# A delta-rule attention with two MoE layers on one core: last second products of a block issued ahead of the next block's first products, and three smaller edits around them

## The chip, the core and the metric

The kernel runs on one core of a Trainium2 chip. Its engines work from queues of their own: TensorE (PE, with its weight loads as PEld), VectorE (DVE), ScalarE (ACT), GpSimd (POOL) and SyncE (SP), which here only issues DMAs. The metric is the device time of one execution in microseconds; lower is better.

## What is computed

The inputs are q, k, v (4 batches, 8 heads, 768 steps, 48 wide), beta, and four weight matrices. All is float32.

```python
k_n = k / (norm(k) + 1e-06)
for t in range(S):                       # state: B, H, 48, 48
    y[:, :, t] = q[:, :, t] @ state
    v_old = k_n[:, :, t] @ state
    state += beta[:, :, t] * outer(k_n[:, :, t], v[:, :, t] - v_old)
x = y.transpose(0, 2, 1, 3).reshape(3072, 384)
h = x @ w_in                             # 384 -> 2048
x = (h * tanh(softplus(h))) @ w_out      # 2048 -> 384, "MoE1"
h = x @ w_in2
out = (h * clip(h + 3, 0, 6) / 6) @ w_out2   # "MoE2"
```

## The kernel before

**Order.** The program for all engines is one static order. `Flow.run` makes it: every part of the work is a generator that yields what it needs next (an event by name, or an engine and a planned duration), and the planner, with a virtual clock for each engine, lets the part with the earliest start plus its penalty (`pen`) go on. The planner's durations are the numbers in the code, such as 0.62 for a cast on ACT. On the chip every engine then runs its list in that order, and waits at semaphores.

**Attention.** The 768 steps are 24 chunks of C = 32, t = 0 to 23. Per chunk, `rec` chains the state products (`S_mm`, L769), the products with it (L719: `ksps` for k, `yps` for q), U (`U_pe`, L729: `ups`, copied to the tile `u` by ACT at L860), MU (`MU_pe`, L739: M times u on top of `yps`) and X (L913, a transpose into the operand of MoE1, copied to `xst` at L929). U needs the inverse of a triangular matrix per chunk and head. For chunks 0 to 7 `quads(0)` and `quads(1)` make these inverses four chunks at a time, and finish them in groups of chunks `ts` with products Q (L626, `qps`); the later ones come from `substs` (L677, L684 on DVE).

**MoE.** `moe` runs 192 units: u = 0 to 95 are MoE1, 96 to 191 MoE2; 6 blocks of 512 tokens times KF = 16 units of 128 hidden columns in each. The first product of a unit (`mm1`, L1080) is 9 matmuls 128x512. Float32 precision is made from split operands: x is xh + xl and w is wh + wl, and the products are xh·wh, xl·wh, xh·wl for each of KD = 3 thirds. The result `hps` goes through the activation function (L1111, or L1207 and L1209 in MoE2), is split into `ghi` (L1086, ACT) and `glo` (L1120 on POOL in MoE1, L1215 on DVE in MoE2), and enters the second product (`mm2`), of 9 matmuls 128x512 (L1101) in MoE1 and 12 matmuls 128x384 (L1234) in MoE2. `mm2` of unit u-2 stands behind `mm1` of unit u. After a block's last `mm2`, `flush1` writes its result to DRAM for MoE2, and `flush2` writes the output: four copies (DVE and ACT, two each) and then four DMAs, one for each batch (L1254).

**Operand of the next block.** `make_x` makes xh (three casts on ACT, L1058) and xl (three subtractions on DVE, L1062) of block n. There is one pair of tiles for xh and xl, so the first cast waits until the last `mm1` of block n-1 is done. Casts and subtractions are asked for in turn: cast 0, subtraction 0, cast 1, and so on.

**Weights.** Raw weights of both layers are converted piece by piece: four steps and the cut of the high part on DVE (L1010 to L1025), the high part as a cast on ACT (L1042, `wih`, `woh`), the low part as a subtraction on DVE (L1045, `wil`, `wol`). MoE1's pieces are converted during the start-up and block 0, those of MoE2 from the end of the attention on.

**Fillers.** `warm` issues matmuls whose result nobody reads, where the planner sees PE idle: 512 columns at L1388 until the first `mm1`, then 256 columns at L1396 until `mm1` of unit 15. Those of L1396 write one bank and wait each for the one before.

**Activation table.** ACT loads the table for the MoE1 function ahead of time (`mish`, L1378).

Of the kernel before, what the change touches and what calls it, by code (L numbers as in the profile page):

```python
# [8 lines left out]
F32 = mybir.dt.float32  # L9
# [117 lines left out]
def tile_delta_rule__moe_mish__moe_hardswish(  # L127
# [38 lines left out]
    with tc.manual_schedule():  # L166
# [408 lines left out]
        def quads(i):  # L575
# [37 lines left out]
            for ts in ((0,), (1,), (2, 3)) if i == 0 else ((0, 1), (2, 3)):  # L613
# [172 lines left out]
        def rec():  # L786


            for t in range(NS):
# [66 lines left out]
                if t:  # L856
                    yield f"MU{t - 1}"
                yield "ACT", 0.5
                u = ut[t] = ap_.tile([128, H, D], F32, tag="u", name="u")
# [191 lines left out]
        def make_x(n, src, last):  # L1051

            if last is not None:
                yield f"mm1.{last}"
            xhl[n] = x = [xp.tile([128, KD, 512], F32R, tag=f"x{p}", name=f"x{p}") for p in "hl"]
            for kk in range(KD):
                yield "ACT", 0.62
                nc.scalar.activation(out=x[0][:, kk, :], in_=src[:, kk, :], func=ACTF.Copy)  # L1058
                if kk == 0 and last is not None:
                    yield 0.8  # L1060
                yield "DVE", 0.55
                nc.vector.tensor_tensor(out=x[1][:, kk, :], in0=src[:, kk, :], in1=x[0][:, kk, :].bitcast(F32),  # L1062
                                        op=ALU.subtract)
                if kk == 0:
                    at = flow.cur
            flow.set(f"mx{n}")
            flow.ev[f"xk{n}"] = at
# [86 lines left out]
        def moe():  # L1154
# [8 lines left out]
            flow.set("moe1")  # L1163
            for u in range(2 * NB * KF):
# [19 lines left out]
                if u >= 2:  # L1184
                    yield from (mm2_second if u - 2 >= NB * KF else mm2_first)(u - 2)
            for u in range(2 * NB * KF - 2, 2 * NB * KF):
                yield from mm2_second(u)
# [52 lines left out]
        def flush2(n):  # L1240
# [3 lines left out]
            for s in range(4):  # L1244
                yield ("DVE", 0.45) if s % 2 else ("ACT", 0.5)
                if s % 2:
                    nc.vector.tensor_copy(out=o[:, s, :], in_=a[s])
                else:
                    nc.scalar.activation(out=o[:, s, :], in_=a[s], func=ACTF.Copy)
            flow.set(f"flush{n}")  # L1250
            yield "SP", 0.3
            for b in range(B):
                r0 = b * S + 128 * i
                nc.sync.dma_start(  # L1254
                    out=out[r0:r0 + 128, :].rearrange("(t s) d -> s t d", s=C),
                    in_=o[C * b:C * (b + 1)],
                )
# [205 lines left out]
```

## Time and profile before

| | us |
|---|---|
| device time, median of 3 runs (lowest, highest) | 1095.82 (1094.92, 1096.76) |
| device time of the profiled execution | 1095.95 |
| its span, first to last instruction | 1094.2 |
| first `mm1` of MoE1 starts | 110.56 |
| first `mm1` of unit 13 starts | 197.32 |
| first `mm1` of MoE2 starts | 674.78 |
| last copy of the output begins | 1087.90 |
| mean granted TensorE clock, share of full | 0.991 |

In a row of the timeline the columns are start, duration, engine, line, operation, output and inputs, shapes, the number of instructions in the row, and in brackets the idle time of the engine just before and what ended it. "128x512 f32 x3" means three such instructions. A matmul's duration is longer than the distance to the next one, since they are pipelined; distances are taken from start to start.

### The profile page before, as it was taken

How to read it: one execution, taken by the hardware profiler on the slowest of the kernel's cores; microseconds unless marked ns; L12 is line 12 of the kernel's file. 1: busy time of each engine (PE TensorE's matmuls, PEld its weight loads, DVE VectorE, ACT ScalarE, POOL GpSimd, SP SyncE). 2: the span in 40 equal slices, each digit the busy share in tenths (PEclk: the TensorE clock that was granted, in tenths of full speed). 3: DMA queues.
4: the chain of work that ended last, by engine and by line, in shares of the span. 5: the costliest groups of instructions: out<-in, count | busy, mean ns of one | idle time of the engine just before them, and what ended most of it. 6: DMA issues, size and time to landing. Idle time of an engine off the chain costs nothing.

```text
span 1094.2 us, 30690 instructions
## 1 busy us (share of the span) xinstructions
PE 1055.4 (96%) x13294; PEld 870.9 (80%) x13329; DVE 664.7 (61%) x1554; ACT 419.0 (38%) x822; POOL 208.3 (19%) x215
## 2 busy tenths in 40 slices
PE   8888999999999999999999998999999999999997
PEld 4666788777778787887887786898989989889896
DVE  6777888868496586938743899834333343333432
ACT  3334544434353344343323434433333342333332
POOL 3110343232333324232322332000000000000000
PEclk9999999999999999999999998999999999999999
DMA  6352434132423333231212543202002020020101
GB/s 150 87 147 51 140 87 112 31 72 38 80 44 74 61 61 82 40 65 28 66 22 73 162 127 116 102 1 58 1 1 58 1 58 1 1 59 1 30 1 29
DMA packets 145799, 66.05 MB, mean 60 GB/s; under 512 B 129760, under 2 KB 132832, under 8 KB 145664
## 3 DMA queue, kind: packets, MB, share of 16 engines
q1 hardware_dynamic: 143456, 63.65, 24.1%
q8 instruction: 104, 1.70, 0.7%
q10 hardware_dynamic: 2208, 0.44, 0.2%
q14 instruction: 31, 0.25, 0.1%
HBM read 50.43 MB, written 13.63 MB: 59 GB/s over the span
## 4 chain that ended last, share of the span: by engine, by line
PE 78%; DVE 16%; issue 2%; ACT 2%; DMA 1%; SPq 1%; POOL 0%; ACTq 0%; DVEq 0%; POOLq 0%
PE hps L1080 30%; PE p L1234 17%; PE o L1101 12%; PE warm L1388 3%; DVE tmp L677 3%; DVE tp L684 3%; PE dsps L769 3%; PE gps L427 2%; PE tps L407 2%; DVE xl L1062 2%; PE qps L626 2%; PE yps L739 1%; PE ups L729 1%; PE ksps L719 1%; PE yps L719 1%
## 5 line engine op out<-in xcount | busy, mean ns | idle before, releaser
L1080 PE MATMUL hps<-xl,wih 128*128 128x512 f32 x576 | 229.3, 398 | 9.8 <-DVE xl L1062 9.8
L1080 PE MATMUL hps<-xh,wih 128*128 128x512 f32 x576 | 229.4, 398 | 6.7 <-ACT g L1111 3.5
L1080 PE MATMUL hps<-xh,wil 128*128 128x512 f32 x576 | 227.1, 394 | 0.0
L1120 POOL TENSOR_TENSOR glo<-g,ghi 128x512 fp32r<-128x512 f32 x96 | 132.5, 1380 | 327.2 <-ACT ghi L1086 273.4
L1209 DVE SCALAR_TENSOR_TENSOR r<-r,hps 128x512 f32<-128x512 f32 x96 | 66.0, 688 | 174.5 <-ACT r L1207 174.5
L1207 ACT ACTIVATE r<-hps,half_c 128x512 f32<-128x512 f32 x96 | 66.1, 689 | 186.7 <-PE hps L1080 186.7
L1080 PEld LDWEIGHTS hps<-xl,wih 128*128 128x128 f32 x576 | 108.4, 188 | 36.4 <-DVE xl L1062 18.1
L1111 ACT ACTIVATE g<-hps 128x512 f32<-128x512 f32 x96 | 57.1, 595 | 197.9 <-PE hps L1080 187.9
L1080 PEld LDWEIGHTS hps<-xh,wih 128*128 128x128 f32 x576 | 108.5, 188 | 30.6 <-ACT g L1111 4.0
L1234 PE MATMUL p<-woh,glo 128*128 128x384 f32 x384 | 129.5, 337 | 0.0
L1234 PE MATMUL p<-woh,ghi 128*128 128x384 f32 x384 | 129.3, 337 | 0.0
L1234 PE MATMUL p<-wol,ghi 128*128 128x384 f32 x384 | 129.0, 336 | 0.0
L1080 PEld LDWEIGHTS hps<-xh,wil 128*128 128x128 f32 x576 | 108.5, 188 | 22.3
L677 DVE TENSOR_TENSOR tmp<-tp,ash 128x126 f32<-128x126 f32 (+22 forms) x248 | 100.8, 406 | 39.1 <-DMA ash<-ad 23.7
L1101 PE MATMUL o<-ghi,woh 128*128 128x512 f32 x288 | 114.7, 398 | 0.0
L1101 PE MATMUL o<-ghi,wol 128*128 128x512 f32 x288 | 114.2, 397 | 0.0
L1215 DVE TENSOR_TENSOR glo<-r,ghi 128x512 fp32r<-128x512 f32 x96 | 66.5, 693 | 59.3 <-ACT ghi L1086 58.8
L684 DVE TENSOR_TENSOR tp<-tp,tmp 128x126 f32<-128x126 f32 (+22 forms) x248 | 82.2, 332 | 7.5 <-DVE tmp L677 0.3
L1086 ACT ACTIVATE ghi<-r 128x512 fp32r<-128x512 f32 x96 | 60.6, 632 | 67.1 <-DVE r L1209 67.0
L1101 PE MATMUL o<-glo,woh 128*128 128x512 f32 x288 | 84.5, 395 | 0.0
L781 DVE TENSOR_TENSOR sbd<-sbd,dsps 48x192 f32<-48x192 f32 x152 | 53.5, 352 | 38.6 <-PE dsps L769 35.4
L1234 PEld LDWEIGHTS p<-woh,ghi 128*128 128x128 f32 x384 | 72.2, 188 | 4.2
(138 smaller groups left out, 1430.1 us busy)
## 6 DMA issues: line engine op xcount, KB each, us to landing
raw<-in_moe_w_in_dram SPq DMA_DIRECT2D x24, 512.0 KB, 4.0
raw<-in_moe_w_out_dram SPq DMA_DIRECT2D x32, 384.0 KB, 3.3
vt<-in_v_dram SPq DMA_DIRECT2D x96, 48.0 KB, 2.2
qpad<-in_q_dram SPq DMA_DIRECT2D x96, 48.0 KB, 2.3
x2d<-x2out SPq DMA_DIRECT2D x6, 768.0 KB, 3.8
x2in<-x2d SPq DMA_DIRECT2D x6, 768.0 KB, 6.0
out_dram<-osb SPq DMA_DIRECT2D x24, 192.0 KB, 3.2
ash<-ad SPq DMA_DIRECT2D x16, 256.0 KB, 3.9
```

The lines of the kernel that those rows point to most:

```text
L677: nc.vector.tensor_tensor(out=tv, in0=x[:, 0:m, j:j + 1].to_broadcast([128, m, n]), in1=a[:, j + 1:C, j:j + 1].rearrange("p i o -> p o i") ...
L684: nc.vector.tensor_tensor(out=x[:, 0:m, j + 1:C], in0=x[:, 0:m, j + 1:C], in1=tv, op=ALU.add)
L781: nc.vector.tensor_tensor(out=o, in0=o, in1=S_part(b, r), op=ALU.add)
L1080: nc.tensor.matmul(out=ps[0], lhsT=w[:, kk, c], rhs=xhl[n][xi][:, kk, :], start=(kk == 0 and x == 0), stop=(kk == KD - 1 and x == 2))
L1086: nc.scalar.activation(out=hi, in_=g, func=ACTF.Copy)
L1101: nc.tensor.matmul(out=acc[i][dc], lhsT=w[:, e, 128 * dc:128 * (dc + 1)], rhs=a, start=(f == 0 and x == 0), stop=(f == KF - 1 and x == 2))
L1111: nc.scalar.activation(out=g, in_=ps, func=ACTF.Mish)
L1120: nc.gpsimd.tensor_tensor(out=lo, in0=g, in1=hi.bitcast(F32), op=ALU.subtract)
L1207: nc.scalar.activation(out=r, in_=ps, func=ACTF.Relu, scale=1.0 / 6.0, bias=half_c)
L1209: nc.vector.scalar_tensor_tensor(out=r, in0=r, scalar=1.0, in1=ps, op0=ALU.min, op1=ALU.mult)
L1215: nc.vector.tensor_tensor(out=lo, in0=r, in1=hi.bitcast(F32), op=ALU.subtract)
L1234: nc.tensor.matmul(out=acc[n][s], lhsT=a[:, c], rhs=w[:, e, :], start=(f == 0 and x == 0), stop=(f == KF - 1 and x == 2))
```

## The change

Five places are edited. (1) In `quads(0)` the chunks 2 and 3 are finished one by one and no longer as a pair. (2) In `rec` the copy of U into `u` waits for the MU product of the chunk before only from chunk 4 on; chunks 1 to 3 put it in tiles of the tag `ghi` instead of the one tile `u`. (3) In `make_x` the three casts are asked for one behind another, and each subtraction is a part of its own that begins when its cast is placed. (4) In `moe` a counter `done` replaces the fixed distance of two units: behind `mm1` of a block's first and last unit, second products are issued up to the unit before, else up to two units before. (5) `flush2` issues one DMA for each of the four copies, directly behind it, in place of the four per batch behind all copies.

```diff
@@ quads @@
-            for ts in ((0,), (1,), (2, 3)) if i == 0 else ((0, 1), (2, 3)):
+            for ts in ((0,), (1,), (2,), (3,)) if i == 0 else ((0, 1), (2, 3)):
@@ rec @@
-                if t:
+                if t >= 4:
                     yield f"MU{t - 1}"
                 yield "ACT", 0.5
-                u = ut[t] = ap_.tile([128, H, D], F32, tag="u", name="u")
+                if 0 < t < 4:
+                    u = gp.tile([128, 512], F32, tag="ghi", name="u")[:, 0:H * D].rearrange("p (h d) -> p h d", h=H)
+                else:
+                    u = ap_.tile([128, H, D], F32, tag="u", name="u")
+                ut[t] = u
                 nc.scalar.activation(out=u, in_=ups.pop(t), func=ACTF.Copy)
@@ make_x @@
-            for kk in range(KD):
-                yield "ACT", 0.62
-                nc.scalar.activation(out=x[0][:, kk, :], in_=src[:, kk, :], func=ACTF.Copy)
+            left, at = [KD], []
+
+            def low(kk):
                 if kk == 0 and last is not None:
                     yield 0.8
                 yield "DVE", 0.55
                 nc.vector.tensor_tensor(out=x[1][:, kk, :], in0=src[:, kk, :], in1=x[0][:, kk, :].bitcast(F32),
                                         op=ALU.subtract)
-                if kk == 0:
-                    at = flow.cur
-            flow.set(f"mx{n}")
-            flow.ev[f"xk{n}"] = at
+                left[0] -= 1
+                at.append(flow.cur)
+                if not left[0]:
+                    flow.set(f"mx{n}")
+                    flow.ev[f"xk{n}"] = at[0]
+
+            for kk in range(KD):
+                yield "ACT", 0.62
+                nc.scalar.activation(out=x[0][:, kk, :], in_=src[:, kk, :], func=ACTF.Copy)
+                flow.add(low(kk), pen=-0.2)
@@ moe @@
+            done = -1
             for u in range(2 * NB * KF):
...
-                if u >= 2:
-                    yield from (mm2_second if u - 2 >= NB * KF else mm2_first)(u - 2)
-            for u in range(2 * NB * KF - 2, 2 * NB * KF):
-                yield from mm2_second(u)
+
+                while done < u - (1 if f in (0, KF - 1) else 2):
+                    done += 1
+                    yield from (mm2_second if done >= NB * KF else mm2_first)(done)
+            while done < 2 * NB * KF - 1:
+                done += 1
+                yield from mm2_second(done)
@@ flush2 @@
+                r0 = 128 * i + C * s
+                nc.sync.dma_start(out=out.rearrange("(b n) d -> b n d", b=B)[:, r0:r0 + C, :], in_=o[:, s, :])
             flow.set(f"flush{n}")
-            yield "SP", 0.3
-            for b in range(B):
-                r0 = b * S + 128 * i
-                nc.sync.dma_start(
-                    out=out[r0:r0 + 128, :].rearrange("(t s) d -> s t d", s=C),
-                    in_=o[C * b:C * (b + 1)],
-                )
```

Since the planner makes the order anew, instructions move in other places too. The lines below L610 shift: L1080 is L1090 in the changed kernel, L1101 is L1111, L1396 is L1405, L1042 is L1046, L1058 is L1076, L1062 is L1066, L1111 is L1121 and L1086 is L1096.

**PE in block 0, between `mm2` of unit 6 and `mm1` of unit 9.** Before:

```order
L1101 MATMUL o_2542<-glo,woh_2238 128x512 [waits Pool_49]
L1101 MATMUL o_2543<-glo,woh_2238 128x512
L1101 MATMUL o_2544<-glo,woh_2238 128x512
L1080 MATMUL hps<-xh,wih_2675 128x512 [waits Activation_49]
L1080 MATMUL hps<-xl,wih_2675 128x512
L1080 MATMUL hps<-xh,wil_2676 128x512
```

And now:

```order
L1111 MATMUL o_2457<-glo,woh_2232 128x512 [waits Pool_49]
L1111 MATMUL o_2458<-glo,woh_2232 128x512
L1111 MATMUL o_2459<-glo,woh_2232 128x512
L1405 LDWEIGHTS ident
L1405 MATMUL warm<-ident 128x256 [waits DVE_49]
L1405 LDWEIGHTS ident
L1405 MATMUL warm<-ident 128x256 [waits PE_49]
```

The last two rows repeat until there are 35 such fillers, and then `mm1` of unit 9 follows. Further groups of 7, 5 and 1 stand ahead of `mm1` of units 11 and 13 and later in the block. Before there were 8 ahead of `mm1` of unit 3, 2 ahead of that of unit 13 and 1 ahead of that of unit 16: 11 in all, and 48 now. Of the fillers at the old L1388 (L1397 now) there were 206, and 197 now.

**PE at the switch from block 0 to block 1 of MoE1.** The rows begin with the last matmul of `mm2` of unit 13. Before:

```order
L1101 MATMUL o_2544<-glo,woh_4041 128x512
L1396 LDWEIGHTS ident
L1396 MATMUL warm<-ident 128x256 [waits Activation_49]
L1080 MATMUL hps<-xh,wih_916 128x512 [waits PE_49,Activation_49]
L1080 MATMUL hps<-xl,wih_916 128x512 [waits DVE_49]
L1080 MATMUL hps<-xh,wil_917 128x512
L1080 MATMUL hps<-xh,wih_916 128x512 [waits Activation_49]
L1080 MATMUL hps<-xl,wih_916 128x512 [waits DVE_49]
```

And now:

```order
L1111 MATMUL o_2459<-glo,woh_4115 128x512
L1111 MATMUL o_2457<-ghi,woh_4115 128x512 [waits Activation_49]
L1111 MATMUL o_2457<-ghi,wol_4116 128x512 [waits DVE_49]
L1111 MATMUL o_2458<-ghi,woh_4115 128x512
L1111 MATMUL o_2458<-ghi,wol_4116 128x512
L1111 MATMUL o_2459<-ghi,woh_4115 128x512
L1111 MATMUL o_2459<-ghi,wol_4116 128x512
L1111 MATMUL o_2457<-glo,woh_4115 128x512 [waits Pool_49]
L1111 MATMUL o_2458<-glo,woh_4115 128x512
L1111 MATMUL o_2459<-glo,woh_4115 128x512
L1090 MATMUL hps<-xh,wih_916 128x512 [waits Activation_49]
L1090 MATMUL hps<-xl,wih_916 128x512 [waits DVE_49]
```

`mm2` of unit 14 has moved ahead of `mm1` of unit 16. Behind it come `mm2` 15, `mm1` 17, `mm1` 18 and `mm2` 16. The ten other switches are alike.

**ACT ahead of the first operand of MoE2.** `woh` and `wih` are converted weights of MoE2, `xh` the operand's high part, `g` and `ghi` those of the last units of MoE1. Before:

```order
L1111 ACTIVATE g<-hps 128x512
L1042 ACTIVATE woh_10623<-cw 128x384
L1086 ACTIVATE ghi<-g 128x512
L1042 ACTIVATE woh_10623<-cw 128x384
L1058 ACTIVATE xh<-x2in 128x512
L1111 ACTIVATE g<-hps 128x512
L1086 ACTIVATE ghi<-g 128x512
L1058 ACTIVATE xh<-x2in 128x512 x2
```

And now:

```order
L1046 ACTIVATE woh_10674<-cw 128x384 x2
L1121 ACTIVATE g<-hps 128x512
L1096 ACTIVATE ghi<-g 128x512
L1046 ACTIVATE wih_10793<-cw 128x512
L1076 ACTIVATE xh<-x2in 128x512 x3
L1121 ACTIVATE g<-hps 128x512
L1096 ACTIVATE ghi<-g 128x512
L1046 ACTIVATE wih_10793<-cw 128x512
```

The three casts stand together, behind the 22nd converted piece of MoE2's weights, and before they stood behind the 21st. The last X product of the attention, behind which the loads of these weights begin, has moved ahead on PE past `mm1` of unit 76 and `mm2` of unit 73, and with pieces of their neighbours past 24 matmuls.

On ACT, a step of the weights (L1018, L1014 before) now stands behind the preload of the table, with two more table loads: one right behind the preload, and one ahead of `g` of unit 0.

## Rows read from the trace of the kernel before

**Rows 1.** The page: busy time, share of the span and instructions of each engine

```profile
PE 1055.4 (96%) x13294; PEld 870.9 (80%) x13329; DVE 664.7 (61%) x1554; ACT 419.0 (38%) x822; POOL 208.3 (19%) x215
```

**Rows 2.** The windows: busy us (instructions) of PE, PEld, DVE, ACT, POOL; clock, DMA share, GB/s

```profile
64.46:110.56 46.10, 41.84 (x1361) 29.91 (x1378) 35.31 (x86) 17.73 (x38) 5.26 (x7) 0.97 0.32 84
110.56:197.32 86.76, 86.00 (x1813) 67.77 (x1813) 70.37 (x169) 39.47 (x89) 33.05 (x28) 1.00 0.41 108
```

**Rows 3.** PE timeline: fillers of both kinds, and products Q, transposes and K

```profile
69.72 1.03 PE L1388 MATMUL warm<-late 128*128 128x512 bf16 x4 [0.16 <-issue]
...
70.68 1.10 PE L626 MATMUL qps<-z,late 32*32 32x16 f32 x64
...
108.06 0.66 PE L407 MATMUL tps<-ident,qpad 128*128 128x128 f32 x4
...
109.30 0.87 PE L719 MATMUL ksps<-sbd,kqt 128*32 128x96 f32 x32
...
128.27 2.56 PE L1396 MATMUL warm<-ident 128*128 128x256 bf16 x8 [0.16 <-ACT vt L315]
```

**Rows 4.** The chain of waits (start, us, what): nine first products without a wait

```profile
176.87 2.26 PE hps L1080 x9
```

**Rows 5.** PE timeline, the first and the fifth switch of a block in MoE1

```profile
217.53 0.47 PE L1080 MATMUL hps<-xh,wih 128*128 128x512 f32 x1 [0.15 <-PE warm L1396]
...
219.69 0.50 PE L1080 MATMUL hps<-xl,wih 128*128 128x512 f32 x1 [1.00 <-DVE xl L1062]
...
221.98 0.40 PE L1101 MATMUL o<-ghi,woh 128*128 128x512 f32 x1
...
601.60 0.39 PE L1080 MATMUL hps<-xh,wih 128*128 128x512 f32 x1
...
606.28 0.63 PE L1101 MATMUL o<-ghi,woh 128*128 128x512 f32 x1
```

**Rows 6.** The windows, behind the fifth switch and at the start of MoE2: columns as in rows 2

```profile
674.40:681.20 6.80, 5.47 (x11) 3.16 (x12) 5.22 (x9) 2.17 (x5) 1.71 (x1) 0.50 0.36 114
606.20:609.60 3.40, 3.40 (x9) 2.67 (x9) 1.87 (x4) 1.75 (x3) 1.28 (x1) 0.50 0.40 120
```

**Rows 7.** POOL and DVE timelines at the first switch

```profile
217.22 1.86 POOL L1120 TENSOR_TENSOR glo<-g,ghi 128x512 fp32r<-128x512 f32 x1 [5.46 <-ACT ghi L1086]
...
218.06 1.58 DVE L1062 TENSOR_TENSOR xl<-xst,xh 128x512 fp32r<-128x512 f32 x1
...
220.69 0.68 DVE L1062 TENSOR_TENSOR xl<-xst,xh 128x512 fp32r<-128x512 f32 x1
```

**Rows 8.** PE and DVE timelines, the switch to MoE2

```profile
674.78 0.80 PE L1080 MATMUL hps<-xh,wih 128*128 128x512 f32 x1 [3.53 <-ACT g L1111]
...
680.73 0.63 PE L1101 MATMUL o<-ghi,woh 128*128 128x512 f32 x1
...
592.46 0.43 DVE L1010 TENSOR_SCALAR cw<-raw 128x512 uint32<-128x512 uint32 x1 [12.82 <-ACT g L1111]
```

**Rows 9.** The windows, from the first converted piece of MoE2 to the 21st

```profile
592.46:673.16 80.70, 77.13 (x330) 62.36 (x328) 75.18 (x130) 33.06 (x60) 27.07 (x18) 0.98 0.44 138
```

**Rows 10.** PE timeline, a switch of a block in MoE2

```profile
882.22 0.40 PE L1080 MATMUL hps<-xh,wih 128*128 128x512 f32 x1
...
882.93 0.50 PE L1080 MATMUL hps<-xl,wih 128*128 128x512 f32 x1 [0.30 <-DVE xl L1062]
```

**Rows 11.** ACT timeline: the load of the table, and what follows it

```profile
90.96 1.28 ACT L1378 ACT_TABLE_LOAD   x1
92.25 0.49 ACT L906 ACTIVATE y<-yps 128x384 f32<-128x384 f32 x1
```

**Rows 12.** DVE and SP timelines at the end, and the view of DMA issues

```profile
1087.90 0.56 DVE L1247 COPY osb<-p 128x384 f32<-128x384 f32 x1 [0.49 <-PE p L1234]
...
1088.52 2.24 SPq L1254 DMA_DIRECT2D out_dram<-osb  x4
...
out_dram<-osb SPq DMA_DIRECT2D x4, 192.0 KB, 3.2
```

## The prediction

> **What bounds the kernel now.** The page comes first: PE is busy for 1055 of the 1094 us, the next engine, DVE, for 665 [rows 1]. So a change pays only where PE stands idle or at half clock, or where PE's own work changes. The windows show that block 0 of MoE1 has next to nothing to give: from the first product at 110.56 to the first product of unit 13 at 197.32 PE is busy for 86.00 of 86.76 us. In the start-up ahead of it, from 64.46 on, PE is busy for 41.84 of 46.10 [rows 2], and the rest is short idle time in front of groups of fillers, put down to "issue" and not to another engine [rows 3]. PE runs through its queue there without waiting for anybody, so that what is added to its queue is paid in full.
>
> PE does stand idle at the switches from block to block. Nine first products without a wait take 2.26 us with the end of the last one, so 2.1 from start to start [rows 4]. At the first switch the nine reach from 217.53 to the next second product at 221.98, which is 4.45, and the idle time is put down to xl [rows 5]. At the switch into MoE2 PE is idle for 3.5 us and then runs nine products in 5.95 [rows 8], with the granted clock at 0.50, that is at 1.2 GHz, for 6.8 us [rows 6]. Within a block of MoE2 there is one short wait, at its first unit [rows 10].
>
> **The change part by part.**
>
> *Fillers, the one part that costs.* The order has 48 fillers of 256 columns in place of 11. Each waits for the one before it. Eight of them took 2.56 us [rows 3], so 0.32 each, and 37 more are +11.8. The other kind loses nine; the row of a group of five (the trace shows four records of it, the order has five) is 1.03 us [rows 3], so 0.2 each, and -1.8. Up to `mm1` of unit 13 both orders put the same other work on PE, and before PE had no wait there that could hide a filler. The sum is **+10.0**. It could be less only if these fillers stand where PE would now wait; but such a wait would be new, and so no gain over before.
>
> *Start-up (edits 1 and 2).* The copy of U of chunk 1 comes ahead of the MU product and no longer behind it. That lets ACT and DVE begin earlier, but PE was not waiting for them, so I book no gain. Ahead of the first `mm1` PE has less to do: 1.8 of fillers, and 2.6 of products Q, K and transposes that now stand behind it (Q 1.10, four transposes 0.66, K 0.87 [rows 3]). If its operand is ready by then, `mm1` begins 4.4 us earlier and nothing is lost; if the operand comes no earlier than before, PE waits for 4.4. The cost is 0 to 4.4, and since the operand hangs on a chain through PE, ACT and DVE for chunk after chunk that edit 2 shortens by part, I take the middle, **+2.0**. The one more cut of Q on DVE (edit 1) is hidden behind DVE's idle time there, 35.31 busy of 46.10 [rows 2].
>
> The two more table loads are 1.28 us each [rows 11] on ACT, which is busy for 17.73 of 46.10 us in that stretch [rows 2]; they are within the same 0 to 4.4. The Trainium skill (page "ScalarE: Activation LUTs", section "What ACT_TABLE_LOAD costs") puts a switch of the table at 2.66 us, the load and a drain of 1.38. Here the next instruction begins 1.29 us after the load's start [rows 11], so the trace agrees with the load and shows no drain behind it. By the page two more would be an estimated 5.3 us of ACT instead of 2.6, and by the same 0 to 4.4 the sum would be up to 2.4 higher.
>
> *The five switches within MoE1 (edits 3 and 4).* PE's loss is the distance from the first product to the next second product less 2.1. It is 2.35 at the first and 2.6 at the fifth [rows 5], and for the three between, read the same way, 1.4, 2.0 and 2.5: together 10.9. The fifth is followed by 3.4 us at half clock [rows 6], which costs 1.7. Now 9 second products, 2.1 us, stand between the last product of the old block and the first of the new one in addition to the 2.1 that stood there already. The casts can begin when the old block's last product ends; three casts and one subtraction behind the third take 4 x 0.65, so some 2.9 with the handovers, and the first subtraction is done at about 1.5. PE asks for the operand at 4.2. All waits go, and no other instruction of DVE stands between the three subtractions. What is late next is `glo` of the last unit, on POOL behind `g` and `ghi`: with 1.86 us for it [rows 7] it is there at about 5, and its product is asked for at 6.2. I leave 0.2 for each switch: **-10.9 - 1.7 + 1.0 = -11.6**.
>
> *The switch into MoE2.* Here xh is late, not xl: its cast stands on ACT behind the 21st converted piece, which DVE cuts until 673.16. DVE makes these pieces from 592.46 on [rows 8] and is busy for 75.18 of the 80.70 us until the 21st [rows 9], so DVE paces them, at 3.8 each. In the new order the cast stands behind the 22nd, +3.8. PE arrives earlier by the loss of the fifth switch, 2.6 + 1.7, and later by the 2.1 of the second product that moved ahead. But the conversion begins sooner: it waits for loads that begin when the attention is done, and the attention's last product moves ahead of 24 matmuls, 5.5 us. So PE's wait becomes 3.5 + 3.8 + 4.3 - 2.1 - 5.5 = 4.0. The nine products behind it lose 3.85 now, 2.1 from the clock and the rest from waits for xl [rows 6, 8]; the clock's part stays, the waits go. The loss of 7.4 becomes 4.0 + 2.1 + 0.2 = 6.3: **-1.1**, with ends at -7.4 (no wait) and +4.4 (no earlier start).
>
> *Five switches in MoE2.* The product that waits starts 0.71 after the one before it in place of 0.23 [rows 10]. The wait goes, five times 0.5: **-2.5**.
>
> *Output (edit 5).* After the last copy SP issues four DMAs in 2.24 us, 3.2 us each to landing [rows 12]. Now three are out by then and only one is left, with as many bytes. Three issues less are 1.7, and the last transfer can meet the one ahead of it, which takes back up to 0.5: **-1.5**. The other five blocks' output is hidden behind products.
>
> **Sum:** +10.0 + 2.0 - 11.6 - 1.1 - 2.5 - 1.5 = -4.7. The profiled execution took 1095.95, 0.13 more than the median, so the forecast is 1091.3 for an execution like that and 1091.1 for the median.
>
> **The rivals.**
>
> A. *The operand of MoE2 is no longer late.* If DVE makes its pieces faster because PE's other waits are gone, the loss of 6.3 that I left there goes too: 1091.1 - 6.3 = 1084.8. For it: DVE stood idle for 12.8 us before the conversion began [rows 8], so an earlier start is usable in full. Against it: 75.18 busy of 80.70 [rows 9]. Chance 0.11.
>
> B. *The conversion begins no earlier.* Its loads may hang on something else than the last attention product. Then the wait grows by the 5.5: 1096.6, the same as before by measurement. For it: the first piece waits for DMAs and four engines in the order. Chance 0.18, of which 0.05 is with a start-up at its upper end, 1098.6 and more.
>
> C. *Slower: DVE is held by POOL, and the subtractions stay late.* At the first switch one subtraction took 1.58 us while POOL worked on `glo` until 219.08, in place of 0.68 [rows 7]. If the three subtractions again meet POOL's `glo` of the old block, which now comes at the same distance behind the last product, and each block in MoE1 loses what it loses now, 11.6 comes back: 1102.7. It turns the sign from 6.9 of the 11.6 on, or 1.3 us per switch. Against it: POOL begins `glo` about 2.2 us behind the last product and ends at 4.0 [rows 7]; a subtraction held until then ends at 4.6 and the last at 5.3, and PE asks for them at 4.9 and 5.6. The Trainium skill ("SBUF — State Buffer", section "Who interferes with whom") says that an instruction of VectorE with two inputs in SBUF contends with one of GpSimd that reads SBUF, and that one of them blocks in full. The row agrees: the subtraction ends 0.56 after POOL does. Chance 0.08.
>
> D. *The change does not move what it says*, in part: the fillers' +10 stands, and half of the gain at the switches goes for other reasons, such as new waits in the attention that the order brings: about 1097. Chance 0.05.
>
> **How the numbers follow.** The forecast's case has 0.58, with its own range from 1087 to 1095 by the start-up's 0 to 4.4 and a few tenths at each switch. About 0.2%, 2.2 us, is what a measurement of this kernel can tell from no change, so faster means below 1093.6 and slower above 1098.0. Faster: 0.51 of the forecast's case and A, 0.62. Same: 0.07 of the forecast's case, 0.13 of B and 0.03 of D, 0.23. Slower: 0.05 of B, 0.08 of C and 0.02 of D, 0.15. The range is 1085 to 1098: it leaves out C, the upper part of B and half of A.
>
> **What would show it.** In the changed kernel: `mm1` of unit 13 some 12 us later than 197.3 (below 205 the fillers cost less than I say; above 212 the start-up waits). No idle time at the first products of blocks 1 to 5, and no half clock behind the fifth switch. Idle time of about 4 us in front of the first `mm1` of MoE2, released by ACT; 9 or more is B, none is A. Each block of MoE2 in 67.0 us in place of 67.6. The last DMA issued within 0.7 us of the last copy. The forecast is wrong if the fillers' rows are shorter than 0.3 each, or if waits come up inside blocks of MoE1.

## The result, and the profile after

The changed kernel takes 1103.24 us in the median of 4 runs, the kernel before 1095.37 in the same comparison: a ratio of 1.0075 with a 95% interval from 1.0056 to 1.0095, so 8.2 us slower (6.1 to 10.4). The forecast was 1091.1, its range ended at 1098, and slower had a chance of 0.15. The forecast was wrong, in sign too.

The page of after, as [rows 1]: the span, and busy us, share and instructions of each engine.

```profile
span 1101.0 us, 30778 instructions
PE 1064.5 (97%) x13357; PEld 874.0 (79%) x13357; DVE 664.4 (60%) x1554; ACT 423.7 (38%) x825; POOL 205.4 (19%) x215
```

PE is busy for 9.1 us more than before, and idle for 36.5 us of the span in place of 38.8: only 2.3 us of idle time went away where some 15 were to go. The starts of `mm1` on PE in both traces (the first of the nine matmuls of a unit; blocks of MoE1 begin at units 16, 32, 48, 64, 80, MoE2 at 96) say where:

| stage | before, us | after, us | difference | forecast |
|---|---|---|---|---|
| span's start to `mm1` 0 | 110.56 | 104.65 | -5.9 | -2.4 |
| `mm1` 0 to 13 | 86.76 | 105.06 | +18.3 | +14.4 |
| `mm1` 13 to 82 | 416.64 | 410.46 | -6.2 | -11.6 |
| `mm1` 82 to 99 | 77.31 | 76.97 | -0.3 | -1.1 |
| `mm1` 99 to 191 | 388.07 | 384.84 | -3.2 | -2.5 |
| `mm1` 191 to the span's end | 14.9 | 19.1 | +4.2 | -1.5 |

**Block 0.** Up to unit 13 the forecast of +12.0 met a difference of +12.4, by two misses that cancel: `mm1` 0 came 3.5 us earlier than forecast, and the stage behind it was 3.9 longer. The 47 fillers of this stage (the 48th stands in block 1) in one row of the groups of instructions (busy us, mean ns, idle time before them), against 0.32 each by [rows 3]:

```profile
L1405 PE MATMUL warm<-ident 128*128 128x256 bf16 x47 | 14.6, 310 | 2.5
```

That is 17.1 us with the idle time, 0.36 each. The windows show why it is more than 0.32: a group of 35 begins at 160.9, and the granted clock falls while it runs (columns as in [rows 2]).

```profile
163.00:166.00 3.00, 2.49 (x10) 0.85 (x9) 2.83 (x8) 2.58 (x9) 0.61 (x1) 1.00 0.61 211
166.00:169.00 3.00, 2.60 (x8) 0.72 (x7) 2.90 (x7) 0.00 (x0) 0.00 (x0) 0.54 0.00 1
169.00:172.00 3.00, 2.60 (x8) 0.73 (x7) 0.04 (x1) 0.00 (x0) 0.00 (x0) 0.50 0.00 0
172.00:175.00 3.00, 2.72 (x9) 1.26 (x7) 0.00 (x0) 0.00 (x0) 0.00 (x0) 0.50 0.00 0
175.00:178.00 3.00, 3.00 (x103) 2.40 (x102) 0.00 (x0) 0.71 (x2) 0.00 (x0) 0.75 0.02 5
```

From 169 to 175 DVE, ACT, POOL and the DMA engines do next to nothing: everybody waits for PE, and PE runs fillers until the group ends at 173.8. Here they hide nothing. In the group as a whole they hide a part: without them (e4 below) PE waits in this place for DVE.

**The switches of MoE1** themselves are as forecast. In the chain of waits of after the nine first products of block 1 run without a wait, where [rows 5] show 1.00 us in front of one of them, and the three subtractions follow one another:

```profile
225.55 2.07 PE hps L1090 x9
...
228.89 1.90 DVE xl L1066 x3
```

But waits have come up inside the blocks. PE's waits from 126 to 620, first before, then after (what waited, for what: us in total, times, longest):

```profile
PE hps L1080 <- DVE xl L1062: 7.3, 10, 1.4
PE hps L1080 <- DVE mt L451: 3.0, 3, 1.8
PE ups L729 <- DVE r L823: 1.0, 1, 1.0
```

```profile
PE hps L1090 <- DVE mt L451: 3.5, 2, 1.8
PE ups L729 <- DVE r L823: 2.4, 4, 0.7
PE tps L407 <- issue: 1.8, 1, 1.8
PE ksps L719 <- DVE sbd L781: 1.5, 4, 0.4
```

The 7.3 us for xl are gone, and the other waits rise from 4.6 to 9.4 (with the rows under 0.3, not shown; "issue" is a wait that the profile puts down to no engine). From `mm1` 18 to `mm1` 82, a stretch that holds switches 2 to 5 and the same products in both kernels, PE is idle for 9.5 us before and for 9.2 after. The chain of after in block 1 shows what stands behind one of the waits: DVE takes the substitution (`tmp`, `tp`) step by step between the pieces of other chunks, `mt` comes behind both, and PE gets it at 276.

```profile
272.24 0.47 DVE nn L341
...
272.79 1.73 POOL nn L387
...
275.64 0.28 DVE tmp L677
275.92 0.21 DVE mt L451
...
276.18 0.96 PE hps L1090 x3
```

POOL has a part in it too. Its 1.73 us on `nn` hold up a small DVE step (L389), with the substitution and `mt` queued behind it. DVE stands idle 0.68 us for it here, 9.1 us in eleven such waits from 200 to 600, and 8.2 in ten before.

**MoE2.** At the switch into it, as [rows 8], PE waits for ACT's `g`, 2.6 us, with two smaller waits for ACT ahead of it (0.6 for `g` and 1.4 for `ghi`), 4.6 in all. The nine products run at half clock in 3.92:

```profile
682.96 1.65 ACT xh L1076 x3
684.62 0.49 ACT g L1121
...
685.15 3.92 PE hps L1090 x9
```

At the switches of blocks in MoE2 the product that waited for 0.30 in [rows 10] follows after 0.23:

```profile
897.90 0.39 PE L1090 MATMUL hps<-xh,wih 128*128 128x512 f32 x1
898.13 0.40 PE L1090 MATMUL hps<-xl,wih 128*128 128x512 f32 x1
```

**The end.** SP's row answers to [rows 12], and behind it stand the windows (DMA share and GB/s are the last two columns):

```profile
1089.48 3.07 SPq L1265 DMA_DIRECT2D out_dram<-osb  x4
```

```profile
1091.00:1094.00 3.00, 0.00 (x0) 0.00 (x0) 0.08 (x1) 0.00 (x0) 0.00 (x0) 1.00 0.24 68
1094.00:1097.00 3.00, 0.00 (x0) 0.00 (x0) 0.00 (x0) 0.00 (x0) 0.00 (x0) 0.61 0.27 100
1097.00:1100.00 3.00, 0.00 (x0) 0.00 (x0) 0.00 (x0) 0.00 (x0) 0.00 (x0) 0.50 0.24 89
```

A quarter of the DMA engines' time, at up to 100 GB/s. Before, the same bytes went out with the share at 0.74 and 0.88 and at 161 and 232 GB/s (windows of before, 1089 to 1091 and 1091 to 1093). From the last copy's start to the span's end it is 6.3 us before and 10.5 after.

### The profile page after: what moved, and what is told of

The parts are those of the page before. It is cut to its first block, busy times and chain, and to the rows that moved or that the text cites. A ratio compares the mean times of both kernels' runs of the same rounds, so it can differ in the third digit from the quotient of the medians.

```text
span 1101.0 us, 30778 instructions
## 1 busy us (share of the span) xinstructions
PE 1064.5 (97%) x13357; PEld 874.0 (79%) x13357; DVE 664.4 (60%) x1554; ACT 423.7 (38%) x825; POOL 205.4 (19%) x215
## 4 chain that ended last, share of the span: by engine, by line
PE 82%; DVE 13%; issue 2%; ACT 1%; DMA 1%; POOL 0%; SPq 0%; DVEq 0%; ACTq 0%
PE hps L1090 31%; PE p L1248 18%; PE o L1111 12%; PE warm L1397 4%; PE dsps L769 3%; DVE tmp L677 2%; PE tps L407 2%; PE gps L427 2%; DVE tp L684 2%; PE yps L739 2%; PE ksps L719 2%; PE ups L729 1%; PE qps L626 1%; DVE cw L1026 1%; PE warm L1405 1%
## 5 line engine op out<-in xcount | busy, mean ns | idle before, releaser
L1090 PE MATMUL hps<-xh,wih 128*128 128x512 f32 x576 | 230.0, 399 | 7.4 <-DVE mt L451 3.5
L1090 PE MATMUL hps<-xl,wih 128*128 128x512 f32 x576 | 226.9, 394 | 0.0
L1090 PE MATMUL hps<-xh,wil 128*128 128x512 f32 x576 | 226.9, 394 | 0.0
L1090 PEld LDWEIGHTS hps<-xh,wih 128*128 128x128 f32 x576 | 108.7, 189 | 30.1 <-ACT g L1121 4.1
L1090 PEld LDWEIGHTS hps<-xh,wil 128*128 128x128 f32 x576 | 108.6, 188 | 23.2
L1121 ACT ACTIVATE g<-hps 128x512 f32<-128x512 f32 x96 | 57.0, 594 | 176.0 <-PE hps L1090 175.9
L1090 PEld LDWEIGHTS hps<-xl,wih 128*128 128x128 f32 x576 | 108.7, 189 | 19.3 <-DVE xl L1066 0.2
L1111 PE MATMUL o<-ghi,woh 128*128 128x512 f32 x288 | 113.6, 394 | 1.4 <-ACT ghi L1096 1.4
L1111 PE MATMUL o<-ghi,wol 128*128 128x512 f32 x288 | 113.9, 395 | 0.0
L1096 ACT ACTIVATE ghi<-r 128x512 fp32r<-128x512 f32 x96 | 60.7, 632 | 75.3 <-DVE r L1223 75.3
L684 DVE TENSOR_TENSOR tp<-tp,tmp 128x126 f32<-128x126 f32 (+22 forms) x248 | 85.0, 343 | 7.3
L1111 PE MATMUL o<-glo,woh 128*128 128x512 f32 x288 | 83.9, 393 | 0.1
```

What stands on the lines that cost most here:

```text
L684: nc.vector.tensor_tensor(out=x[:, 0:m, j + 1:C], in0=x[:, 0:m, j + 1:C], in1=tv, op=ALU.add)
L1090: nc.tensor.matmul(out=ps[0], lhsT=w[:, kk, c], rhs=xhl[n][xi][:, kk, :], start=(kk == 0 and x == 0), stop=(kk == KD - 1 and x == 2))
L1096: nc.scalar.activation(out=hi, in_=g, func=ACTF.Copy)
L1111: nc.tensor.matmul(out=acc[i][dc], lhsT=w[:, e, 128 * dc:128 * (dc + 1)], rhs=a, start=(f == 0 and x == 0), stop=(f == KF - 1 and x == 2))
L1121: nc.scalar.activation(out=g, in_=ps, func=ACTF.Mish)
```

## The experiments

Ratios are to the kernel before, run beside each. A single profile carries about 3 us of chance: in ten traces with the old start-up `mm1` 0 begins between 105.8 and 110.6 (the kernel before has the latest), in six with edits 1 and 2 between 101.3 and 104.8. Stretches of 3.4 us at clock 0.50 add to it, and they strike in other places from trace to trace: from `mm1` 18 to `mm1` 82 the four kernels with edits 1 to 4 (after, e1, e4, e8) take 382.5, 386.2, 384.4 and 384.3 us with none, two, one and one of them, and 382.5 to 382.8 each when half of that time is taken off. So parts are priced by ratios, and traces say where. The kernels are e1 to e14. "Fillers" are those of the second loop (L1405 after).

**Edit 5 apart.** e1 is the change without it, e2 the kernel before with it alone, e5 the same with two batches in each DMA in place of four.

```
-    nc.sync.dma_start(out=out.rearrange("(b n) d -> b n d", b=B)[:, r0:r0 + C, :], in_=o[:, s, :])
...
+for b in range(B):
+    nc.sync.dma_start(out=out[...].rearrange("(t s) d -> s t d", s=C), in_=o[C * b:C * (b + 1)])
```

> The changed kernel with edit 5 undone: four output DMAs per batch behind the four copies, as before. Theory S (the new form of the output DMA is slow: 99 GB/s at the end, and 10.5 us from the start of the last copy to the end of the span, 6.3 before): the end comes back, -4.2 us, 1099.0 (1098.5 to 1099.8), and the last first product stays 2.6 later than in the kernel before. Rival (the late end has to do with what PE and DVE do, not with the form of the DMA): 1103.

Measured: 1100.24 us, 1.0059 (1.0039 to 1.0079). The rest of the change is slower by itself. Against 1.0075 that gives back 1.8 us, with some 3 on either side, which does not tell 4.2 from nothing; in the trace `mm1` 191 to the end is 14.9 again in place of 19.1. In its trace the clock stands at 0.50 in the long group of fillers too.

```
+    nc.sync.dma_start(out=out.rearrange("(b n) d -> b n d", b=B)[:, r0:r0 + C, :], in_=o[:, s, :])
```

> The kernel before with edit 5 alone. Theory S: +4.2 us, 1099.6, and about 10.5 us from the start of the last copy to the end. My prediction's step (fewer issues behind the last copy): -1.5, 1093.9.

Measured: 1100.14, 1.0043 (1.0026 to 1.0060), so +4.7 us. Edit 5 is a loss, of the size that the trace shows at the end (4.2).

```
+    for h in range(2):
+        nc.sync.dma_start(out=out...[2 * h:2 * h + 2, r0:r0 + C, :], in_=o[64 * h:64 * h + 64, s, :])
```

> The kernel before with edit 5, each DMA of a copy cut into two of two batches each (slowest dimension 2 in place of 4, the same bytes and the same rows). Theory S in its sharp form (a DMA runs on as many of the 16 DMA engines as its slowest dimension has entries: DMA share 0.25 with 4): the share falls to 0.13, the rate to about 50 GB/s, and 786 KB take 16 us: about 18 us from the last copy to the end, 1095 + 12 = 1107. Rival (rows scattered over four batches are slow, or the issue behind each copy): no more than one us of change from edit 5 alone, 1100.

Measured: 1106.47, 1.0113 (1.0071 to 1.0155), from two runs. Its windows at the end:

```profile
1094.00:1097.00 3.00, 0.00 (x0) 0.00 (x0) 0.00 (x0) 0.00 (x0) 0.00 (x0) 0.50 0.13 50
1097.00:1100.00 3.00, 0.00 (x0) 0.00 (x0) 0.00 (x0) 0.00 (x0) 0.00 (x0) 0.50 0.13 50
```

Two batches in a DMA: 0.13 of the engines' time, as much as 2 of 16, and 50 GB/s. Four batches: 0.25, as much as 4 of 16, and 100 GB/s. So the share goes with the number of batches, the slowest dimension of the destination, and not with the number of DMAs: a block's output is four DMAs of 192 KB before and after, and eight of half of that in e5. (The traces give the share of all 16 engines and do not name those that work.) The Trainium skill ("DMA: Bandwidth & Descriptors", section "Why a DMA increments its semaphore by 16 and not by 1") says that a DMA takes the largest number of engines, up to 16, that divides the slowest dimension of both its patterns. The shares in the traces agree at 4 and at 2; the old DMAs, with 32 there, reach a share of 0.88.

**Fillers apart.** e4 and e8 have edits 1 to 4 without edit 5. e4 has no second loop of fillers; e8 has another price for a filler in the planner (0.11 us is written there; one takes 0.32 by [rows 3]).

```
-            while "mm1.15" not in flow.ev and flow.cur < 300.0:
+            while False:
```

> As the first of these (edit 5 undone), and without the 48 fillers of 256 columns, which nobody reads. They take 47 x 0.36 = 17 us of PE's queue in block 0. If they delay everything behind them, theory F: -13 to -17, about 1084, and the first product of unit 13 near 194. If they only fill time in which PE would have waited for DVE, the rival: -5 at most, 1094 or more, with new idle time in front of the first products of units 9, 11 and 13. Half clock in block 0 would show if they kept the clock up.

Measured: 1088.12, 0.9943 (0.9927 to 0.9960). Against 1.0059 with them (e1) the fillers cost 12.7 us, though 47 of them take 16.8 us in the trace of e1. Its stage from `mm1` 0 to 13 is 12.8 longer than that of e4, so some 4 us of the fillers stood where PE would have waited: e4 waits 2.5 us ahead of `mm1` 9 and 1.0 ahead of `mm1` 11 (PE's waits from 100 to 196):

```profile
PE hps L1090 <- DVE mt L451: 3.5, 2, 2.5
```

The expectation's rival named this idle time; it shows in part.

```
-                yield "PE", 0.11, 0
+                yield "PE", 0.33, 0
```

> The changed kernel with edit 5 undone, and the planner told 0.33 us for a filler of 256 columns, as measured, in place of 0.11. Its order then has 18 of them. Theory F: 30 fillers less are -10, and no run is long enough for the clock to fall, which saves up to 5: between the run with edit 5 undone (1.006) and that without fillers (0.994), near 0.996. Rival (the half clock of block 0 comes from something else in that place): half clock stays in the windows from 150 to 180 us, and the ratio is 0.999 or more.

Measured: 1088.04, 0.9936 (0.9913 to 0.9960). With its price right the planner places 18 in place of 48, and these cost nothing that can be measured.

e9 is the kernel before without its fillers of that loop.

```
-            while "mm1.15" not in flow.ev and flow.cur < 300.0:
+            while False:
```

> The kernel before without the fillers of its own second loop (11 of them). If each is paid in full, as it is in the changed kernel, 11 x 0.32 = 3.5 us go: about 1091.6, a ratio of 0.997. Together with the run of edits 3 and 4 alone without fillers (0.9925) this says what edits 3 and 4 are worth by themselves: about 0.995. The other theory: the fillers of before stand where the planner expected PE to wait and cost nothing, 1095, a ratio of 1.000; then edits 3 and 4 are worth 0.9925 in full.

Measured: 1094.35, 0.9997 (0.9986 to 1.0009). The 11 fillers of before cost nothing that can be measured, the 48 of after do: a filler costs what it stands in the way of.

**Edits 1 to 4 apart.** e3 has edits 3 and 4 alone, with the fillers that the planner then places (38), e7 the same without fillers. Seen from the change:

```
-            for ts in ((0,), (1,), (2,), (3,)) if i == 0 else ((0, 1), (2, 3)):
+            for ts in ((0,), (1,), (2, 3)) if i == 0 else ((0, 1), (2, 3)):
...
-                if 0 < t < 4:
-                    u = gp.tile(...)
```

> The kernel before with edits 3 and 4 alone (order of the second products, order of casts and subtractions). Its order has 38 fillers of 256 columns, where before had 11 and the full change has 48. Theory L (in blocks 1 to 4 of MoE1 a loop through DVE's substitution and its DMAs sets the pace, so that PE gets back at the switches what it then waits inside the blocks): fillers 27 x 0.36 = +9.7, switches in MoE1 -12.6, given back +5.3, into MoE2 -0.4, in MoE2 -3.2: -1.2, 1094.2, with block periods 1 to 3 of 98 to 99 us as before. Rival P (the give-back comes with edits 1 and 2): -6.5, 1088.9, with block periods of 96 to 97.

Measured: 1093.72, 0.9993 (0.9968 to 1.0017), near theory L, with block periods 1 to 3 of 99.5, 99.2 and 98.3.

```
-            while "mm1.15" not in flow.ev and flow.cur < 300.0:
+            while False:
```

> The kernel before with edits 3 and 4 alone, and no fillers of 256 columns (38 in the run with edits 3 and 4). Theory F (fillers delay everything behind them, 0.33 each): -12.5, of which the loop in blocks 1 to 4 takes nothing back since its first group moves as well: 1082 to 1085, ratio 0.989. Rival: edits 1 and 2 bring forward the first product, which this kernel lacks; then it is slower than the run without fillers and with all of edits 1 to 4 (0.994) by up to 4: 0.998.

Measured: 1087.50, 0.9925 (0.9901 to 0.9949). So 38 fillers cost 7.4 us here (0.9993 - 0.9925), and edits 3 and 4 by themselves gain 7.9 against the kernel before without fillers (0.9925 / 0.9997 = 0.9928, e9 to e7). Theory F had 12.5 for the fillers. PE's waits from 126 to 620 in this kernel:

```profile
PE hps L1086 <- DVE mt L451: 4.1, 5, 1.8
PE tps L407 <- issue: 3.7, 2, 1.9
PE ups L729 <- DVE r L823: 1.2, 2, 0.8
PE hps L1086 <- DVE pt L642: 1.2, 1, 1.2
PE ksps L719 <- DVE sbd L781: 1.1, 3, 0.4
```

No wait for xl is left, and the sum of all, 12.2 with two smaller rows, is what the kernel before without fillers has, 12.6, of which 7.5 for xl. The waits have moved from the switches into the blocks.

e14 is e9 with edit 3 alone, casts and subtractions; its expectation calls this edit 4 and the second products edit 3, the other way round than in "The change".

```
+            for kk in range(KD):
+                yield "ACT", 0.62
+                nc.scalar.activation(out=x[0][:, kk, :], in_=src[:, kk, :], func=ACTF.Copy)
+                flow.add(low(kk), pen=-0.2)
```

> Edit 4 alone (each third of the operand cast and subtracted one behind another), no fillers of the second loop, second products where they stood before. The subtractions come earlier, but PE asks for them 2.1 us behind the old block's last product, and the first is done at about 1.5 and the third at 2.9: a part of the xl waits goes, 1 of some 2.2 at each of ten switches at most: between 1091 and 1094, a ratio of 0.997 to 0.999. If the gain of edits 3 and 4 (0.9925) is edit 4's alone, 0.9925; if edit 4 does nothing without edit 3, 0.9997.

Measured: 1095.49, 1.0001 (0.9981 to 1.0021). These casts and subtractions alone gain nothing against 0.9997: the trace has 4.7 us of waits for xl left from 126 to 620 and twice the waits for `mt`:

```profile
PE hps L1086 <- DVE mt L451: 6.1, 6, 1.9
PE hps L1086 <- DVE xl L1062: 4.7, 5, 1.3
```

The gain needs the second products ahead of the new block's first (edit 4 in "The change"). Whether they would gain it alone was not run.

e10 is e9 with edits 1 and 2 alone.

```
+            for ts in ((0,), (1,), (2,), (3,)) if i == 0 else ((0, 1), (2, 3)):
...
+                if 0 < t < 4:
+                    u = gp.tile(...)
```

> Edits 1 and 2 alone (the copy of U into the free buffer, Q's first chunk in four parts) on the kernel before, no fillers of the second loop. If the earlier first product (6 us in the profile of the changed kernel) is kept to the end, 6 us below the kernel before without fillers: about 1086, a ratio of 0.991. If block 0 gives it back because its operands come at the pace of the attention and not of PE, about 1091.5, a ratio of 0.997.

Measured: 1101.04, 1.0044 (1.0028 to 1.0061). Neither expectation held: edits 1 and 2 alone cost 5.1 us. `mm1` 0 begins 2.9 us earlier than in the kernel before without fillers, and the stretch from there to `mm1` 82 is 9.3 longer. Beside edits 3 and 4 they cost less: 0.9943 against 0.9925, 2.0 us, with intervals that overlap.

**What holds the blocks of MoE1.** e6 is e4 with a second buffer for `ash`, so that the load of the next group's matrices goes on while DVE works on one.

```
+    if g % 2:
+        a = cvp.tile([128, 512, 2], F32, tag="r1", name="ash")...
+    else:
+        a = ap_.tile([128, C, C], F32, tag="ash", name="ash")
```

> The changed kernel with edit 5 undone and without the 48 fillers, as in the run without fillers (ratio 0.994), and with a second tile for the matrices that the substitution on DVE reads, so that the next group's load need not wait for the end of the group before. Theory L (the loop through substitution and its load holds blocks 1 to 4): DVE's idle time for that load (6.8, 1.8, 7.9, 1.8, 5.4 us in the changed kernel, 24 in all) goes, PE's waits for DVE in the blocks, 11 us, are halved, blocks 1 to 3 take 96 to 97 us in place of 99 to 100: -6, ratio 0.989. Rival: DVE's own steps or PE hold the blocks, no change, 0.994.

Measured: 1103.78, 1.0107 (1.0061 to 1.0152), 18 us slower than e4. The planner put DVE's work in another order, and PE then waits for `sbd` for 14.7 us, 14 times. It speaks against the load as the cause no more than for it, since the order changed with it.

So the next pair leaves every instruction of every engine in its place and shortens the substitution alone, by leaving out three quarters of its columns: e12 is e9, e13 is e7 with this edit.

```
-                    yield "DVE", 0.16 + 0.00095 * n * m
+                    cost = 0.16 + 0.00095 * n * m; m = (m + 3) // 4; yield "DVE", cost
```

> The kernel before without the fillers of its second loop, every instruction in the same place on every engine, but the forward substitution on DVE (lines 677 and 684) does only a quarter of its columns: this part of the inverses is left out. DVE loses about 75 of its 350 us between 126 and 620. Theory: PE's waits inside the blocks of MoE1 hang on DVE's substitution; then the 4.6 us of them go and the waits at the switches stay, 1090.5, a ratio of 0.9955 (without this cut 0.9997). Rival: the waits hang on the order in which DVE has its other work, not on how long the substitution takes: 1094.5, a ratio of 0.9995.

> Edits 3 and 4 alone, no fillers of the second loop, and the same cut of the substitution to a quarter of its columns, every instruction in the same place. Theory: the waits that edits 3 and 4 brought into the blocks of MoE1 (12 us by PE's waits between 126 and 620, 4 of them there before) go, and the full gain at the switches shows: about 1079.5, a ratio of 0.986, so 0.99 against the run before with the same cut. Rival: the waits stay, 1087, a ratio of 0.9925.

Measured: 1086.01, 0.9896 (0.9858 to 0.9934) without, and 1074.49, 0.9796 (0.9765 to 0.9827) with edits 3 and 4. Both gained more than the theory had: 11 us against e9 in place of 4.6 and 14 us against e7 in place of 7.5, each with some 4 on either side, though the substitution lost only 51 us of DVE's time. So its length holds PE, with and without edits 3 and 4. The ratio of the two is 0.9899, so edits 3 and 4 gain 11.1 us here, where it was 7.9; with some 5 and 3 on either side these times alone do not tell the two gains apart. The windows below do. DVE's rows from 126 to 620, first of e7, then of e13:

```profile
L677 DVE TENSOR_TENSOR tmp<-tp,ash 128x126 f32<-128x126 f32 (+22 forms) x248 | 101.4, 409 | 35.0 <-DMA ash<-ad 19.6 <-POOL tp L670 8.9
L684 DVE TENSOR_TENSOR tp<-tp,tmp 128x126 f32<-128x126 f32 (+22 forms) x248 | 81.9, 330 | 7.2
```

```profile
L677 DVE TENSOR_TENSOR tmp<-tp,ash 128x24 f32<-128x24 f32 (+23 forms) x248 | 69.5, 280 | 31.9 <-DMA ash<-ad 16.5 <-POOL tp L670 8.9
L684 DVE TENSOR_TENSOR tp<-tp,tmp 128x24 f32<-128x24 f32 (+23 forms) x248 | 62.3, 251 | 7.2
```

And the windows from `mm1` 18 to `mm1` 82, which hold the same products on PE in all four kernels: e9 and e7 with the whole substitution, then e12 and e13.

```profile
225.95:611.56 385.61, 376.29 (x6066) 301.20 (x6064) 259.11 (x731) 151.48 (x332) 125.74 (x124) 1.00 0.29 59
227.94:610.13 382.19, 374.91 (x6066) 302.55 (x6065) 261.35 (x736) 151.86 (x332) 125.13 (x123) 1.00 0.29 62
```

```profile
226.01:605.18 379.17, 374.85 (x6066) 301.12 (x6065) 217.98 (x731) 151.52 (x332) 122.25 (x124) 1.00 0.29 61
225.51:595.88 370.37, 370.37 (x6066) 300.66 (x6065) 214.68 (x726) 151.48 (x332) 122.36 (x123) 1.00 0.30 64
```

Edits 3 and 4 bring this stretch from 385.6 to 382.2 us with the whole substitution, and from 379.2 to 370.4 with the short one. One stretch of 3.4 us at half clock falls into each of the first three and none into e13, so without the clock the gains are 3.4 and 7.1. PE's idle time goes from 9.3 to 7.3 in the first pair and from 4.3 to nothing in the second.

With 28% of the substitution's time gone (183 to 132 us) PE is never idle there in e13; in e12 it still waits at the switches. In e7 DVE is busy for 68% of the stretch, and yet how long its substitution takes is what holds PE inside the blocks. How it does so is read from the chain alone: what PE waits for stands in DVE's queue among the substitution's steps. DVE's own waits, for the load of `ash` (16.5 us in the row above) and for POOL's `nn` (11.8 us from 200 to 600), are still there in e13 and cost PE nothing. No run shows what shortening them would bring with the whole substitution.

**A faster kernel.** e11 is e7 with two of the last four output DMAs on ACT's queue.

```
+    (nc.scalar if i == NB - 1 and b >= 2 else nc.sync).dma_start(
```

> Edits 3 and 4 alone, no fillers of the second loop, and of the last four output DMAs two issued by ACT's queue beside SP's. If the issue by SP (0.56 us each) holds the end, two issues less are 1.1 us: 1086.4, a ratio of 0.9915 against 0.9925 without it. If the transfers hold it, 1087.5 as without it.

Measured: 1086.05, 0.9916 (0.9890 to 0.9942), the lowest median of the kernels that do the whole computation; e7 (0.9925) and e8 (0.9936) lie within its interval. The 1.4 us between its median and that of e7 are within the intervals too; that the queue brings them is not shown.

## Why the prediction was wrong, point by point

The forecast was 4.7 us faster, and the result is 8.2 slower. The step that failed most is "All waits go": edits 3 and 4 gained 7.9 us in place of 15.2, because PE then waited inside the blocks for DVE. The second is the output (edit 5), a loss of 1.8 to 4.7 in place of a gain of 1.5.

The runs make a path from one kernel to the other, one part at a time; the differences of their ratios, times 1095, are the measured prices.

| part | forecast | measured | from |
|---|---|---|---|
| fillers of the second loop | +11.8 | +12.4 | e4 to e1 +12.7, before to e9 -0.3 |
| edits 1 and 2, with nine fillers of the other loop fewer | +0.2 | +2.0 | e7 to e4 |
| edits 3 and 4 | -15.2 | -7.9 | e9 to e7 |
| edit 5 | -1.5 | +1.8 to +4.7 | e1 to after, before to e2; 4.2 in the trace |

Each step has an interval of some 2 to 3 us on either side. With 1.8 for edit 5 the path ends at +8.3, as it must: the differences of the ratios add up to that of the direct comparison, +8.2, so this confirms no price.

**Output.** This step failed in sign. It counted issues and bytes, "only one is left, with as many bytes". What it left out is the shape: the batch became the slowest dimension, 4 in place of 32, and the share of the DMA engines fell from 0.88 to 0.25. In the other five blocks the output is hidden behind products, as forecast: `mm1` 99 to 191 takes 384.84 us with the old output (e1) and with the new one.

**Switches within MoE1.** "All waits go" held at the switches and nowhere else. The forecast listed what is late next at the switch (`glo`), found it early enough, and left 1.0; it did not ask the same of the blocks. PE comes earlier to the attention's products there, by what the switches no longer take, while `mt`, `r` and `sbd` come at DVE's pace. Its last sentence named this, "if waits come up inside blocks of MoE1", and rival D gave it 0.05. DVE's pace was read in the start-up and ahead of MoE2 [rows 2, 9], not in blocks 1 to 4, though waits for `mt` and `r` of up to 1.8 us stood there before. e12 and e13 show the cause: with a shorter substitution nothing holds PE there, and edits 3 and 4 gain 7.1 us from `mm1` 18 to `mm1` 82 in place of 3.4. The half clock behind the fifth switch did go, since the windows of after have 1.00 from 604 to 620, against 0.50 in [rows 6]. But to book its 1.7 us as a gain was luck: e9, with the old order there, has no half clock in that place and one at 361, and e1, with the new order, has two, at 369 and 464.

**Fillers.** The sum was right within a microsecond by the runs, and that is in part luck, since its terms were not. It paid 37 more fillers 0.32 each. The 11 of before cost nothing, so all 48 count; at half clock one takes 0.43 from start to start; and some 4 us of them stood where PE would have waited, as the forecast allowed for ("such a wait would be new").

**Start-up.** `mm1` 0 began 5.9 us earlier in place of 2.4, but products moved behind it, and PE paid for them there. Beside edits 3 and 4 the measured +2.0 has some 3 us on either side and so does not differ from the +0.2 that was booked. Without them the cost is +5.1, more than the booked upper end of 4.4. Why edits 1 and 2 cost more alone is not settled.

**MoE2.** Its blocks gained 3.2 in place of 2.5: 66.92 us each against 67.57, where 67.0 was named. The switch into it gained 0.3 in place of 1.1. PE's wait for ACT rose to 4.6 us in all, where 4.0 was named, and the half clock there, which the forecast had as staying, fell from 6.8 us to 3.4. Rivals A (no wait) and B (9 or more) fell.

**Rivals.** C put the sign on POOL's `glo` and on subtractions that stay late; the time fits its 1102.7, the mechanism does not, since the three subtractions run in 1.90 us together.

## What to carry to other kernels

When the bytes of a DMA are regrouped, compare the slowest dimension of both patterns before the number of issues: four DMAs of the same size took a quarter of the engines' time where they had taken up to 0.88. A wait that is taken away can come back at the next thing that is late, so ask what paces the work between the waits as well, and test it with a kernel in which the order stays and only the suspect gets shorter. Filler work that is planned at a third of its true price fills more than the gap that it was meant for; with the true price 18 were placed in place of 48 and cost nothing that could be measured.

## What was not expected of the hardware

The granted clock fell to 0.50, 1.2 GHz, while PE ran one chained matmul after another without a longer pause: 35 fillers of 256 columns, each waiting for the one before, 0.33 us from start to start at full clock and 0.43 at half. In the first 5 us of the group it was still at 1.00, and behind it at 0.75 and 1.00. In the kernel with 18 fillers in place of 48 (e8) it stays at 1.00 from 100 to 200, and in e3, whose longest group is 18, from 150 to 180. That the chain is what lowered it is not shown: e7, which has none of these fillers, fell to 0.50 at 165.6 for 3.4 us, behind a wait of PE of 1.9.

Transfers with four batches took 0.25 of the DMA engines' time at about 100 GB/s, and with two 0.13 at 50, so an estimated 25 for each engine that works, in runs of 1,536 bytes.
